# Inverting a running product from the product itself instead of scanning the inverses

## The chip, the cores and the metric

The kernel runs on one core of one Trainium2 chip. Its time is the device time of a run in microseconds; a profile of one execution tells where it goes. The engines are TensorE (PE, with its weight loads as PEld), VectorE (DVE), ScalarE (ACT), GpSimd (POOL) and SyncE (SP); transfers run on queues that SP, POOL and ACT issue to.

## The reference

A gated linear recurrence with complex gates feeds a feed-forward layer with a squared ReLU:

```
mag = sqrt(a_re^2 + a_im^2);  scale = min(mag, 0.999) / (mag + 1e-6)
a = (a_re + i a_im) * scale                       # per batch, head, step, channel
for t in range(S):
    S_t = a_t * S_(t-1) + k_t v_t^T               # S complex, 48 x 48 per head
    y_t = q_t . real(S_t)
x = y as (B*S, H*D)                               # 3072 x 384
out = relu(x @ w_in)^2 @ w_out                    # 384 -> 2048 -> 384
```

B = 4 batches, H = 8 heads, S = 768 steps, D = 48 channels, all in float32; the weights arrive as float64.

## The kernel before

**Algorithm.** With P_t the running product of the gates, the real part of q_t . S_t is a sum over s <= t of (q_t P_t)(k_s / P_s) v_s, so each unit becomes matrix products: q times P, k times 1/P, a masked score matrix, and a carried state. P starts from 2^59 in each sequence so that it stays in range over 768 steps. The kernel works in real numbers: 1/P is conj(P)/|P|^2, so what k needs beside the parts of P is 1/|P|^2.

**Units.** The 3072 steps are cut into `NU` = 6 units of 512 steps. A unit's operands lie as 128 partitions of four consecutive steps (`W` = 4), in two halves `z` of four heads. Units 0 and 1 are handled in groups of two heads (`apply(z, p, 1)`), later ones a half at a time (`apply(z, 0, 2)`).

**`chain(n)` of a unit.** `roots` and `normalise` compute 1/mag by Ln and Exp with a Newton step and scale the gates; `inner` multiplies the four steps of a partition into prefix products (VectorE). `totals` transposes each partition's last product on TensorE, `scan` multiplies over the partitions (VectorE), `back` transposes the result: `xn[:, 0]`, `xn[:, 1]` hold the product up to each partition. `inverse` computes 1/|prefix|^2 inside each partition (Square, Ln, Exp on ScalarE, a Newton step on VectorE); its last column goes through `factors`: a transposing matmul (line 1061), a scan of products along the partitions (`tensor_tensor_scan`, line 1082, with tests of growth and size at 1086 and 1090), a transposing matmul back (line 1104): `xn[:, 2]` is the running product of inverses. `twist` multiplies k by the inverse inside the partition (line 994). `apply` multiplies the prefixes by `xn` (1245, 1249), k by `xn[:, 2]` (1252), then forms the products for k and for q (1259). `gather` moves those for k by DMA (line 1299).

**`pairs(n)`.** For each pair of heads: transposes of q's and k's products (on TensorE through line 1358 in units 0 and 1, copied out by ScalarE at 1362; by VectorE and DMA later), scores (1376) with a mask (1379), state sums (1404, 1413, 1415), the mix with v (1428, 1432), its copy (1438) and DMA into `xT` (1446).

**`dense(n, grp)`.** First layer at line 1468, ReLU and square on ScalarE (1499, 1500), second layer at 1514 in unit 0; later units use line 1565 and combinations of `w2` blocks made once at 1555. The float64 weights are fetched in pieces and converted by ScalarE (795, 799) and VectorE (801, 805, 808) during unit 0.

**Order.** Each operation is recorded as a `step` with an engine, an assumed duration, reads, writes and a rank; `Plan.order` replays them greedily (an engine takes the ready step of lowest rank) and the program is emitted in that order. Each engine runs its own queue in order. Ranks: `DENSE` = 3, `CHAIN` = 2, `PAIR` = 1; a step of `ahead` comes just before the unit's other chain steps, `late` is the rank of the inverse and of `apply`. Accumulated sums (`sums`, `grow`, `total`) are tested in `verdict`; where a test fails, a general branch of the program computes everything anew.

Of the kernel before, what the change touches and what calls it, by code (L numbers as in the profile page):

```python
# [588 lines left out]
def fast_path(ctx, tc, q, k, v, a_re, a_im, moe_w_in, moe_w_out, out, flag):  # L589
# [6 lines left out]
    C = 128  # L596
# [13 lines left out]
    CUT = C // 2  # L610
# [32 lines left out]
    x = sb("x", NM * (C + 1)).rearrange("p (m c) -> p m c", m=NM)  # L643
    xe = sb("xe", NM)
    txs = [sb(f"tx{j}", 3 * 24).rearrange("p (r g) -> p r g", r=3) for j in range(2)]
    ce = sb("ce", 2 * NM).rearrange("p (r m) -> p r m", r=2)
    cx = sb("cx", NM)
    xn = sb("xn", 3 * DM).rearrange("p (r n) -> p r n", r=3)
# [15 lines left out]
    NS = 10  # L664
    sums = sb("sums", NU * NS).rearrange("p (n j) -> p n j", n=NU)
    grow = sb("grow", NU * 2 * NM).rearrange("p (n j m) -> p n j m", n=NU, j=2)
    total = sb("total", B * NM).rearrange("p (b m) -> p b m", b=B)
# [30 lines left out]
    pool.memset(col, 1.0)  # L698
    pool.memset(txs[0].rearrange("p r (m k) -> p r m k", k=8)[:, 0, :, 0], 1.0)
# [179 lines left out]
    def chain(n):  # L879
# [12 lines left out]
        def third(lo, hi):  # L892

            return [("xn", 2, i) for i in range(lo // 64, (hi + 63) // 64)]

        def roots(z):
# [11 lines left out]
            else:  # L908
# [6 lines left out]
                out=f0, in_=m2, func=AF.Ln), first)  # L915
# [10 lines left out]
        def normalise(z):  # L926
            f0, f1, _, t = col[z]
            step("ACT", ac(Y), key(z, 3), key(z, 0), lambda: act.activation(
                out=f0, in_=t, func=AF.Copy, scale=0.999), first)
            step("ACT", ac(Y), key(z, 3), key(z, 1), lambda: act.activation(  # L930
                out=f1, in_=t, func=AF.Copy, scale=-1e-6, bias=1.0), first)
            step("DVE", tt(Y), key(z, 0, 1), key(z, 0), lambda: dve.scalar_tensor_tensor(
                out=f0, in0=f0, scalar=1.0, in1=f1, op0=ALU.min, op1=ALU.mult), first)
            a2 = A[z].rearrange("p (r x) -> p r x", r=2)
            step("DVE", tt(Z), key(z, 0), [("a", z)], lambda: dve.tensor_tensor(  # L935
                out=a2, in0=a2, in1=f0.unsqueeze(1).to_broadcast([C, 2, Y]),
                op=ALU.mult), first)
            check("ACT", ac(Y), key(z, 3), [], lambda: act.activation(
                out=junk[:, 0:Y], in_=t, func=AF.Square, saturate=False,
                accum_out=sums[:, n, 2 + z:3 + z]), first)  # L940
            if n == 0:
                check("ACT", ac(Y), key(z, 2), [], lambda: act.activation(
                    out=junk[:, 0:Y], in_=col[z][2], func=AF.Copy, saturate=False,
                    accum_out=sums[:, n, z:z + 1]), first)
# [25 lines left out]

        def inverse(z):
            f0, f1, d, t = col[z]
            rk = late[z]
            step("ACT", ac(Z), [("a", z)], key(z, 0, 1), lambda: act.activation(
                out=ff[z][:, 0:Z], in_=A[z], func=AF.Square), rk)
            step("DVE", tt(Y), key(z, 0, 1), key(z, 2), lambda: dve.tensor_tensor(
                out=d, in0=f0, in1=f1, op=ALU.add), rk)
            step("ACT", ac(Y), key(z, 2), key(z, 0), lambda: act.activation(
                out=f0, in_=d, func=AF.Ln), rk)
            step("ACT", ac(Y), key(z, 0), key(z, 1), lambda: act.activation(  # L980
                out=f1, in_=f0, func=AF.Exp, scale=-1.0), rk)
            step("DVE", tt(Y), key(z, 1, 2), key(z, 3), lambda: dve.scalar_tensor_tensor(
                out=t, in0=d, scalar=-1.0, in1=f1, op0=ALU.mult, op1=ALU.mult), rk)
            step("DVE", tt(Y), key(z, 1, 3), key(z, 3), lambda: dve.scalar_tensor_tensor(
                out=t, in0=t, scalar=2.0, in1=f1, op0=ALU.add, op1=ALU.mult), rk)
            xh = xn.rearrange("p r (h d) -> p r h d", h=H)[:, :, ts(z, HH)]
            t4 = t.rearrange("p (h c d) -> p h c d", h=HH, c=W)
            step("ACT", ac(Y // W), key(z, 3), third(z * HH * D, (z + 1) * HH * D),
                 lambda: act.copy(out=xh[:, 2], in_=t4[:, :, W - 1]), rk)

        def twist(z):
            t = col[z][3]
            kk = QK[z][:, Y:2 * Y]
            step("DVE", tt(Y), key(z, 3) + [("qk", z)], [("k", z)], lambda: dve.tensor_tensor(
                out=kk, in0=kk, in1=t, op=ALU.mult), late[z])
# [54 lines left out]

        def factors(lo, hi, rk):

            rows = [(m, max(lo - C * m, 0), min(hi - C * m, C)) for m in range(lo // C, (hi - 1) // C + 1)]
            ks = third(lo, hi)
            b = trs[slot["tr"] % 2]
            ps = bank[b][:, 0:DM].rearrange("p (m t) -> p m t", m=NM)
            slot["tr"] += 2

            def go():
                for m, p0, p1 in rows:  # L1060
                    pe.matmul(ps[p0:p1, m], lhsT=xn[:, 2, C * m + p0:C * m + p1], rhs=ident,
                              start=True, stop=True)
            step("PE", 0.12 * len(rows), ks, [(b,)], go, rk)

            groups = [([m for m, p0, p1 in rows if (p0, p1) == (0, C)], 0, C)] + [
                ([m], p0, p1) for m, p0, p1 in rows if (p0, p1) != (0, C)]

            def scan_x():
                for ms, p0, p1 in groups:
                    if not ms:  # L1070
                        continue
                    sl = slice(ms[0], ms[-1] + 1)
                    if fresh:
                        dve.memset(x[p0:p1, sl, 0], SCALE ** -2)
                    else:
                        dve.tensor_copy(out=x[p0:p1, sl, 0], in_=cx[p0:p1, sl])
                    for hf in range(2):
                        t0, t1 = hf * CUT, (hf + 1) * CUT
                        if hf and cross:
                            dve.memset(x[p0:p1, sl, t0], SCALE ** -2)  # L1080
                        for m in ms:
                            dve.tensor_tensor_scan(
                                out=x[p0:p1, m, t0 + 1:t1 + 1], data0=ps[p0:p1, m, t0:t1],
                                data1=mask[p0:p1, 0:CUT], initial=x[p0:p1, m, t0:t0 + 1],
                                op0=ALU.mult, op1=ALU.bypass)
                        dve.scalar_tensor_tensor(
                            out=grow[p0:p1, n, hf, sl], in0=x[p0:p1, sl, t0], scalar=2.0 ** 124,
                            in1=x[p0:p1, sl, t1], op0=ALU.mult, op1=ALU.is_ge)
                        if (ends and hf) or (cross and not hf):
                            dve.tensor_scalar(  # L1090
                                out=total[p0:p1, ps_[0][2], sl], in0=x[p0:p1, sl, t1],
                                scalar1=2.0 ** 114, scalar2=None, op0=ALU.is_le)
                    if not ends:
                        dve.tensor_copy(out=cx[p0:p1, sl], in_=x[p0:p1, sl, C])
            kx = [("x", i) for _, _, i in ks]
            check("DVE", sum(0.5 + 0.6 * len(ms) for ms, _, _ in groups if ms), [(b,)] + kx, kx,
                  scan_x, rk)

            b2 = trs[(slot["tr"] + 1) % 2]
            ps2 = bank[b2][:, 0:DM]  # L1100

            def go2():
                for m, p0, p1 in rows:
                    pe.matmul(ps2[:, C * m + p0:C * m + p1], lhsT=x[p0:p1, m, 0:C],
                              rhs=ident[p0:p1, p0:p1], start=True, stop=True)
            step("PE", 0.12 * len(rows), kx, [(b2,)], go2, rk)
            step("ACT", ac(hi - lo), [(b2,)], ks, lambda: act.copy(
                out=xn[:, 2, lo:hi], in_=ps2[:, lo:hi]), rk)
# [106 lines left out]

        def squares(j):
            for r in range(2):
                check("ACT", ac(Y), [(("qk", "k")[r], j)], [], lambda r=r: act.activation(
# [7 lines left out]
        def apply(z, p, np):  # L1226
# [20 lines left out]
            for r, op in ((0, ALU.subtract), (1, ALU.add)):  # L1247
# [3 lines left out]
            lo = (z * HH + 2 * p) * D  # L1251
            step("DVE", tt(n1), third(lo, lo + nh * D), [("k", z)], lambda: dve.tensor_tensor(
                out=qk[:, 1], in0=qk[:, 1], in1=over(2), op=ALU.mult), late[z])
# [497 lines left out]
```

## Time and profile before

| | |
|---|---|
| median of 3 runs | 722.57 us (722.43 to 722.73) |
| span of the profiled execution | 722.6 us |
| PE busy | 647.1 us |
| weight loads busy | 579.3 us |
| DVE busy | 576.7 us |
| ACT busy | 359.1 us |
| POOL busy | 176.1 us |
| transfers | 79.53 MB, mean 110 GB/s |

The span runs from the first to the last instruction of one profiled execution; it is the only time that this execution has, and it equals the runs' median within 0.05 us. Busy times of PE come from pipelined records: a record's duration overlaps that of its neighbour, so the pace is read from starts or from the chain of waits. A float32 matmul appears as two records. Each engine runs its instructions in order, so an instruction that waits holds up all behind it.

### The profile page before, as it was taken

What the parts mean: (1) busy time and instruction counts of PE and PEld (TensorE: products, weight loads), DVE (VectorE), ACT (ScalarE), POOL (GpSimd) and SP (SyncE); (2) the same over time, 40 slices, a digit from 0 to 9 for tenths busy, and PEclk for the clock granted to TensorE, in tenths of its full rate; (3) what the DMA queues carried; (4) which work ended last, traced back from release to release, by engine and by line L of the source; (5) the groups of instructions that cost most, each with busy time, mean ns of one, the idle gap of its engine ahead of it and who ended that gap; (6) DMA issues with size and microseconds to landing.
All of it is one profiled execution on the core that took longest, in us unless ns stands there. A gap on an engine that the chain in (4) does not pass through costs nothing.

```text
span 722.6 us, 11635 instructions
## 1 busy us (share of the span) xinstructions
PE 647.1 (90%) x4118; PEld 579.3 (80%) x4118; DVE 576.7 (80%) x1188; ACT 359.1 (50%) x579; POOL 176.1 (24%) x333
## 2 busy tenths in 40 slices
PE   0017798999998999999999999999999999999996
PEld 0006687677777799999999899999998989999996
DVE  6998899799776589879799588999788997347621
ACT  6792557965366523347713559424569142122230
POOL 6504154051500003305006241024050033032100
PEclk9999899999998999999999999999999999999999
DMA  9732259220530002646006772017560045297400
GB/s 287 239 128 65 57 114 275 104 66 10 161 116 19 4 12 74 179 122 165 0 12 177 165 153 65 1 36 186 157 163 9 1 128 129 51 325 266 153 1 27
DMA packets 56356, 79.53 MB, mean 110 GB/s; under 512 B 10944, under 2 KB 38464, under 8 KB 56288
## 3 DMA queue, kind: packets, MB, share of 16 engines
q0 software_dynamic: 15232, 40.72, 18.7%
q1 hardware_dynamic: 36928, 32.98, 17.9%
q10 hardware_dynamic: 4128, 4.98, 2.6%
q8 instruction: 35, 0.57, 0.4%
q14 instruction: 33, 0.27, 0.1%
HBM read 48.76 MB, written 4.72 MB: 74 GB/s over the span
## 4 chain that ended last, share of the span: by engine, by line
PE 76%; DVE 14%; ACT 3%; DMA 2%; SPq 2%; issue 1%; POOL 0%; DVEq 0%
PE d L1468 29%; PE d L1565 26%; PE sc L1376 5%; PE d L1514 4%; PE tr L1404 3%; PE yp L1428 3%; DVE f L954 3%; PE yp L1432 2%; DVE aq L935 1%; PE tr L1013 1%; PE d L1358 1%; DMA KC<-f 1%; DVE f L1259 1%; DVE aq L960 1%; DVE f L1245 1%
## 5 line engine op out<-in xcount | busy, mean ns | idle before, releaser
L1468 PE MATMUL d<-xT,w 128*128 128x256 f32 x1056 | 236.9, 382 | 0.6 <-DMA xT<-yt 0.6
L1468 PEld LDWEIGHTS d<-xT,w 128*128 128x128 f32 x1056 | 199.3, 191 | 27.8 <-issue 1.1
L1565 PE MATMUL d<-w,g 128*128 128x192 f32 x768 | 132.2, 327 | 0.0
L1565 PEld LDWEIGHTS d<-w,g 128*128 128x128 f32 x768 | 124.9, 190 | 1.1 <-issue 0.7
L1499 ACT ACTIVATE g<-d 128x512 f32<-128x512 f32 x88 | 52.4, 595 | 127.0 <-PE d L1468 113.3
L1299 POOL DMA_DIRECT2D KC<-f x160 | 78.9, 501 | 121.7 <-DVE f L1259 55.9
L1580 DVE TENSOR_TENSOR g<-g 128x512 f32<-128x512 f32 x64 | 43.6, 688 | 35.4 <-ACT g L1500 20.3
L1565 PE MATMUL d<-T,g 128*128 128x192 f32 x384 | 66.8, 326 | 0.0
L875 POOL DMA_DIRECT2D v<-in_v_dram x80 | 46.5, 588 | 82.6 <-PE yp L1428 28.5
L1526 POOL DMA_DIRECT2D out_dram<-ot x22 | 12.4, 562 | 207.5 <-DVE ot L1589 136.0
L1565 PEld LDWEIGHTS d<-T,g 128*128 128x128 f32 x384 | 62.9, 190 | 0.0
L1500 ACT ACTIVATE g<-g 128x512 f32<-128x512 f32 x96 | 60.6, 631 | 3.1
L1376 PE MATMUL sc<-QT 96*128 96x128 f32 x368 | 49.9, 292 | 2.1 <-ACT QT L1362 2.1
L1376 PEld LDWEIGHTS sc<-QT 96*128 96x128 f32 x368 | 46.5, 204 | 4.9 <-ACT QT L1362 2.9
L1259 DVE TENSOR_TENSOR f<-aq 128x384 f32<-128x384 f32 (+1 forms) x64 | 45.1, 752 | 0.6
L1245 DVE TENSOR_TENSOR f<-aq,xn 128x384 f32<-128x384 f32 (+1 forms) x64 | 44.7, 748 | 0.0
L1514 PE MATMUL d<-w,g 128*128 128x384 f32 x128 | 43.3, 487 | 0.7 <-DVE w L808 0.7
L1438 ACT COPY yt<-yp 112x512 f32<-112x512 f32 x24 | 26.3, 1097 | 25.2 <-PE yp L1432 25.2
L1589 DVE TENSOR_TENSOR ot<-ot,d 128x192 f32<-128x192 f32 x64 | 21.7, 349 | 21.5 <-PE d L1565 21.1
L954 DVE TENSOR_TENSOR f<-aq 128x384 f32<-128x384 f32 x72 | 36.9, 553 | 0.9
L1514 PEld LDWEIGHTS d<-w,g 128*128 128x128 f32 x128 | 23.5, 190 | 15.2 <-DVE w L808 1.1
L1013 PE MATMUL tr<-perm,xn 128*128 128x128 f32 x36 | 6.1, 303 | 32.7 <-ACT xn L969 31.6
(194 smaller groups left out, 1019.5 us busy)
## 6 DMA issues: line engine op xcount, KB each, us to landing
QT<-aq SPq DMA_DIRECT2D x128, 64.0 KB, 2.1
f<-in_moe_w_in_dram POOLq DMA_DIRECT2D x8, 768.0 KB, 7.9
f<-in_moe_w_out_dram POOLq DMA_DIRECT2D x8, 768.0 KB, 6.4
KC<-f POOLq DMA_DIRECT2D x104, 48.0 KB, 2.2
out_dram<-ot POOLq DMA_DIRECT2D x22, 192.0 KB, 2.2
QT<-aq ACTq DMA_DIRECT2D x64, 64.0 KB, 2.3
v<-in_v_dram POOLq DMA_DIRECT2D x80, 48.0 KB, 2.7
xT<-yt SPq DMA_DIRECT2D x36, 96.0 KB, 2.4
```

Of the source, the lines that this page charges most:

```text
L875: lambda i=i, c=c, src=src: pool.dma_start(out=t[32 * c:32 * c + 32, i], in_=src[c]), vrank, 32 * 1536, 4.0,
L954: dve.tensor_tensor(out=f, in0=a[:, :, :, c - 1], in1=a[:, j, :, c].unsqueeze(1).to_broadcast([C, 2, HH, D]), op=ALU.mult)
L1245: lambda j=j, r=r: dve.tensor_tensor(out=f4[:, j, r], in0=a[:, r], in1=over(j), op=ALU.mult), late[z])
L1259: lambda j=j, r=r, o=o: dve.tensor_tensor(out=o[:, :, :, r * D:(r + 1) * D], in0=qk[:, j], in1=a[:, r], op=ALU.mult), late[z])
L1299: lambda i=i, c=c, queue=queue: queue.dma_start(out=kc[32 * c:32 * c + 32, i], in_=nat[32 * i:32 * i + 32, c]),
L1376: pe.matmul(sa[:, j], lhsT=T[:, j, 1, h], rhs=T[:, j, 0, h], start=True, stop=True)
L1468: pe.matmul(ps, lhsT=w1[:, f // FP, m, ts(f % FP, C)], rhs=xT[:, n % 2, m, ts(grp, G)], start=(m == 0), stop=(m == NM - 1))
L1499: act.activation(out=o, in_=ps, func=AF.Relu)
L1500: act.activation(out=o, in_=o, func=AF.Square)
L1514: pe.matmul(ps, lhsT=gt[:, f % 2, ts(i, C)], rhs=w2[:, f], start=(f == 0), stop=(f == NF - 1))
L1565: pe.matmul(bank[b][:, 0:DH], lhsT=g4[:, r, j], rhs=w(j), start=first and j == 0, stop=last and j == NT - 1)
L1580: step("DVE", tt(4 * C), gk(x0, h) + gk(x1, h), gk(o, h), lambda: dve.tensor_tensor(out=g4[:, o, sl], in0=g4[:, x0, sl], in1=g4[:, x1, sl] ...
```

## The change

The running product of inverses (`factors`, `inverse`, `twist`, the third row of `xn`) goes. Instead, `apply` inverts |P|^2 of the complete product, element by element, with its own Square, Ln, Exp and Newton step. To keep Ln and Exp in range, each partition has a level `lv`, one over the sum of the squares of its `xn` row, taken by a Square with accumulation and a reciprocal; Ln reads it as a scale, and the Newton step and the last multiplication of k carry it as well. In `roots` the factor 0.999 moves into Ln's scale, so that one of two Copies of `normalise` goes, and the other reads the Exp's result ahead of the Newton step. A check of unit 0 (the sum over `m2`) gets a later rank. The sums of squares of k are taken before k is scaled. The tests of `grow` and `total` are replaced by sums read out behind the new Exp.

```diff
         def roots(z):
...
             step("ACT", ac(Y), key(z, 2), key(z, 0), lambda: act.activation(
-                out=f0, in_=m2, func=AF.Ln), first)
+                out=f0, in_=m2, func=AF.Ln, scale=CLIP ** -2), first)
...
+            step("ACT", ac(Y), key(z, 1), key(z, 0), lambda: act.activation(
+                out=f0, in_=f1, func=AF.Copy, scale=-1e-6 / CLIP, bias=1.0), first)
             step("DVE", tt(Y), key(z, 2, 3), key(z, 3), lambda: dve.scalar_tensor_tensor(
-                out=t, in0=m2, scalar=-0.5, in1=t, op0=ALU.mult, op1=ALU.mult), first)
+                out=t, in0=m2, scalar=-0.5 * CLIP ** -2, in1=t, op0=ALU.mult, op1=ALU.mult), first)
...
         def normalise(z):
-            step("ACT", ac(Y), key(z, 3), key(z, 0), lambda: act.activation(
-                out=f0, in_=t, func=AF.Copy, scale=0.999), first)
-            step("ACT", ac(Y), key(z, 3), key(z, 1), lambda: act.activation(
-                out=f1, in_=t, func=AF.Copy, scale=-1e-6, bias=1.0), first)
-            step("DVE", tt(Y), key(z, 0, 1), key(z, 0), lambda: dve.scalar_tensor_tensor(
-                out=f0, in0=f0, scalar=1.0, in1=f1, op0=ALU.min, op1=ALU.mult), first)
+            step("DVE", tt(Y), key(z, 0, 3), key(z, 0), lambda: dve.scalar_tensor_tensor(
+                out=f0, in0=t, scalar=1.0, in1=f0, op0=ALU.min, op1=ALU.mult), first)
...
-        def inverse(z):
...
-        def twist(z):
...
-        def factors(lo, hi, rk):
...
+        step("ACT", ac(Y) + 0.2, [("xn", r, z) for r in range(2) for z in range(2)], [("tot",)],
+             lambda: act.activation(out=junk, in_=xn.rearrange("p r n -> p (r n)"),
+                                    func=AF.Square, scale=LOW, saturate=False,
+                                    accum_out=tot[:, n:n + 1]), ahead)
+
+        def level():
+            dve.reciprocal(out=lv[:, n, 0:1], in_=tot[:, n:n + 1])
+            dve.tensor_scalar(out=lv[:, n, 1:2], in0=lv[:, n, 0:1], scalar1=-UP * UP,
+                              scalar2=None, op0=ALU.mult)
+        check("DVE", 0.16, [("tot",)], [("lv", n)], level, ahead)
...
         def apply(z, p, np):
...
-            lo = (z * HH + 2 * p) * D
-            step("DVE", tt(n1), third(lo, lo + nh * D), [("k", z)], lambda: dve.tensor_tensor(
-                out=qk[:, 1], in0=qk[:, 1], in1=over(2), op=ALU.mult), late[z])
+            f0, f1, d, t = [own[:, i * n1:(i + 1) * n1] for i in range(4)]
+            pp = a.rearrange("p r h c d -> p r (h c d)")
+            step("ACT", ac(2 * n1), [("a", z)], kf[0], lambda: act.activation(
+                out=own[:, 0:2 * n1].rearrange("p (r x) -> p r x", r=2), in_=pp,
+                func=AF.Square, scale=UP), late[z])
+            step("DVE", tt(n1), kf[0], kf[1], lambda: dve.tensor_tensor(
+                out=d, in0=f0, in1=f1, op=ALU.add), late[z])
+            step("ACT", ac(n1), kf[1] + [("lv", n)], kf[0], lambda: act.activation(
+                out=f0, in_=d, func=AF.Ln, scale=lv[:, n, 0:1]), late[z])
+            check("ACT", ac(n1) + 0.1, kf[0], kf[0], lambda: act.activation(
+                out=f1, in_=f0, func=AF.Exp, scale=-1.0,
+                accum_out=sums[:, n, 10 + 2 * z + p:11 + 2 * z + p]), late[z])
+            step("DVE", tt(n1), kf[0] + kf[1], kf[1], lambda: dve.scalar_tensor_tensor(
+                out=t, in0=d, scalar=lv[:, n, 0:1], in1=f1, op0=ALU.mult, op1=ALU.mult), late[z])
+            step("DVE", tt(n1), kf[0] + kf[1], kf[1], lambda: dve.scalar_tensor_tensor(
+                out=t, in0=t, scalar=-2.0, in1=f1, op0=ALU.add, op1=ALU.mult), late[z])
+            step("DVE", tt(n1), kf[1] + [("qk", z)], [("k", z)],
+                 lambda: dve.scalar_tensor_tensor(
+                     out=qk[:, 1].rearrange("p h c d -> p (h c d)"), in0=t,
+                     scalar=lv[:, n, 1:2], in1=qk[:, 1].rearrange("p h c d -> p (h c d)"),
+                     op0=ALU.mult, op1=ALU.mult), late[z])
...
         def rest(*zs):
             for z in zs:
-                inverse(z)
-            factors(zs[0] * HH * D, (zs[-1] + 1) * HH * D, late[zs[0]])
-            for z in zs:
-                twist(z)
                 squares(z)
```

More of the change, by code (lines that the diff above doesn't have):

```diff
@@ L609, in fast_path @@
     G = L // 2
-    CUT = C // 2
+    UP = 2.0 ** 4
+    LOW = 2.0 ** -1
+    CLIP = 0.999
     Z = 2 * HH * W * D
@@ L663, in fast_path @@
     mask = sb("mask", C)
-    NS = 10
+    NS = 14
+    lv = sb("lv", NU * 2).rearrange("p (n j) -> p n j", n=NU)
+    tot = sb("tot", NU)
     sums = sb("sums", NU * NS).rearrange("p (n j) -> p n j", n=NU)
-    grow = sb("grow", NU * 2 * NM).rearrange("p (n j m) -> p n j m", n=NU, j=2)
-    total = sb("total", B * NM).rearrange("p (b m) -> p b m", b=B)
     odd = sb("odd", NF)
@@ L698, in fast_path @@
     pool.memset(col, 1.0)
+    pool.memset(sums, 0.0)
     pool.memset(txs[0].rearrange("p r (m k) -> p r m k", k=8)[:, 0, :, 0], 1.0)
@@ L943, in normalise @@
                     out=junk[:, 0:Y], in_=col[z][2], func=AF.Copy, saturate=False,
-                    accum_out=sums[:, n, z:z + 1]), first)
+                    accum_out=sums[:, n, z:z + 1]), (CHAIN, 0.2))
         def inner(z):
@@ L969, in inner @@
                  lambda: act.copy(out=xh[:, 0:2], in_=a[:, :, :, W - 1]), ahead)
-        def inverse(z):
[L972 to L989, printed above, removed]
-        def twist(z):
[L992 to L995, printed above, removed]
         for fn in (roots, normalise, inner):
@@ L1049, in totals @@
             step("DVE", 0.12, [("ce",)], [("e", j)], start, ahead)
-        def factors(lo, hi, rk):
[L1053 to L1108, printed above, removed]
@@ L1644, in collect @@
         def collect():
-            for lo, hi, top_ in ((0, 2, 60), (2, 4, 12), (4, NS, 20)):
+            for lo, hi, top_ in ((0, 2, 60), (2, 4, 12), (4, 8, 7), (8, 10, 20), (10, NS, 60)):
                 dve.tensor_scalar(out=ok[:, :, lo:hi], in0=sums[:, :, lo:hi],
                                   scalar1=2.0 ** top_, scalar2=None, op0=ALU.is_le)
+            wide = sums[:, :, 10:NS]
+            dve.tensor_tensor(out=wide, in0=wide, in1=lv[:, :, 1:2].to_broadcast([C, NU, NS - 10]),
+                              op=ALU.mult)
+            dve.tensor_scalar(out=wide, in0=wide, scalar1=-2.0 ** 118, scalar2=None,
+                              op0=ALU.is_ge)
+            dve.tensor_reduce(out=good[:, 1:2], in_=wide, axis=AXY, op=ALU.min)
             dve.tensor_reduce(out=good[:, 0:1], in_=ok, axis=AXY, op=ALU.min)
-            dve.tensor_reduce(out=good[:, 1:2], in_=grow, axis=AXYZ, op=ALU.min)
-            dve.tensor_reduce(out=good[:, 2:3], in_=total, axis=AXY, op=ALU.min)
             dve.tensor_reduce(out=most, in_=odd, axis=AX, op=ALU.max)
```

9 lines of the change are left out of this document (2 added, 7 removed).

## The prediction

> **What bounds the kernel now.** I read the page first: totals, the slices, the chain.
>
> ```profile
> span 722.6 us, 11635 instructions
> PE 647.1 (90%) x4118; PEld 579.3 (80%) x4118; DVE 576.7 (80%) x1188; ACT 359.1 (50%) x579; POOL 176.1 (24%) x333
> PE   0017798999998999999999999999999999999996
> DVE  6998899799776589879799588999788997347621
> PE 76%; DVE 14%; ACT 3%; DMA 2%; SPq 2%; issue 1%; POOL 0%; DVEq 0%
> ```
>
> The span, 722.6 us, stands at the median of the runs (722.57), so the sum is made against it. TensorE is idle for 75.5 us, nearly all of it early: in the first slices it does nothing while VectorE is full. The chain agrees: mostly PE, with a DVE part. Next the stages, as windows of PE alone (columns: stage, its length, PE busy with its records, granted clock, DMA share, GB/s).
>
> ```profile
> 0.00:103.70 103.70, 45.45 (x332) 0.97 0.51 150
> 103.70:135.00 31.30, 27.55 (x120) 1.00 0.76 208
> 135.00:213.00 78.00, 77.28 (x419) 1.00 0.34 92
> 213.00:222.00 9.00, 4.86 (x49) 0.99 0.09 23
> 222.00:232.00 10.00, 10.00 (x62) 0.67 0.01 2
> 232.00:253.00 21.00, 19.33 (x91) 1.00 0.04 9
> 253.00:715.60 462.60, 462.60 (x3053) 1.00 0.39 107
> ```
>
> So there are three regimes. Up to 103.7 us VectorE's unit 0 sets the pace. From 253 us PE never waits: there only PE's own work counts, and VectorE time saved is worth nothing. Between them lies one hole at 213 to 222 us.
>
> **PE's own work.** The change drops both transposing stages of the inverse's scan (`factors`, lines 1061 and 1104). How long they hold PE is read from the chain of waits (start, length), since a record's mean overlaps its neighbours.
>
> ```profile
> 168.24 0.67 PE tr L1061 x6
> 168.91 3.89 PE d L1468 x18
> 172.79 0.67 PE tr L1104 x6
> L1061 PE MATMUL tr<-ident,xn 128*128 128x128 f32 (+1 forms) x38 | 6.4, 300 | 1.5 <-ACT xn L989 1.5
> ```
>
> Six records each per unit (38 = 8 for unit 0 and 30 for five units), 0.67 + 0.67 us a unit. Units 1 to 5 run after 135 us, where PE is full: 5 x 1.34 = **6.7 us** come off the path. Nothing is added on PE. Unit 0's are in the part that VectorE bounds.
>
> **VectorE and ScalarE, whole kernel.** Groups of instructions (busy us, mean ns; then idle before):
>
> ```profile
> L994 DVE TENSOR_TENSOR aq<-aq,f 128x768 f32<-128x768 f32 x12 | 11.4, 954 | 0.2
> L982 DVE SCALAR_TENSOR_TENSOR f<-f 128x768 f32<-128x768 f32 x12 | 11.4, 952 | 5.3 <-ACT f L980 5.3
> L1252 DVE TENSOR_TENSOR aq<-aq,xn 128x384 f32<-128x384 f32 (+1 forms) x16 | 12.0, 751 | 0.0
> L1082 DVE TENSOR_TENSOR_SCAN x<-tr,x,mask 128x64 f32<-128x64 f32 (+1 forms) x38 | 11.1, 336 | 0.9
> L1259 DVE TENSOR_TENSOR f<-aq 128x384 f32<-128x384 f32 x32 | 16.0, 553 | 0.3
> L1086 DVE SCALAR_TENSOR_TENSOR grow<-x 128x3 f32<-128x3 f32 (+2 forms) x18 | 2.9, 161 | 0.6
> L930 ACT ACTIVATE f<-f 128x768 f32<-128x768 f32 x12 | 9.9, 828 | 0.0
> L989 ACT COPY xn<-f 128x192 f32<-128x192 f32 x12 | 4.2, 346 | 6.6 <-DVE f L984 6.4
> L1031 ACT ACTIVATE e<-tr 128x384 f32<-128x384 f32 x6 | 3.1, 511 | 0.0
> L1218 ACT ACTIVATION_READ_ACCUMULATOR junk<-aq 128x1 f32 x24 | 4.5, 187 | 0.0
> ```
>
> Gone from VectorE: the twist 11.4, the multiplication by the running inverse 12.0, scans 11.1 and their tests 2.9: 37.4 us. Added: one last scaled multiplication of k per group, as wide as L1252 (12.0), and twelve one-column operations (reciprocal, factor; nearest row 161 ns: 1.9). The three other operations of the inverse stay, but in units 0 and 1 cut in halves: 24 x 0.553 for 12 x 0.953, +1.8. Net -21.7 us. ScalarE: one Copy of two goes (9.9), L989 goes (4.2); the Square with a sum over xn comes (6 x (0.83 + 0.19) = 6.1) and 16 sums read out behind Exp (3.0): about -5 us. The reciprocal has no row; between 0.16 and 0.95 us each it moves unit 0 by under a microsecond, and I take 0.16. After 253 us all this is cover: PE has dense work queued.
>
> Ln now takes its scale from a tile, of which no row exists either. The Trainium skill ("ScalarE: Activation LUTs", What ACT_TABLE_LOAD costs) states some 93 ns more for such a pointer operand; by it unit 0's four Ln would end 0.4 us later in all, and no run here shows it.
>
> **Unit 0, where VectorE bounds.** Timeline rows of before (start, length, engine, line):
>
> ```profile
> 11.75 0.96 DVE L923 SCALAR_TENSOR_TENSOR f<-f 128x768 f32<-128x768 f32 x1
> 15.55 0.95 DVE L932 SCALAR_TENSOR_TENSOR f<-f 128x768 f32<-128x768 f32 x1
> 35.56 0.36 DVE L1122 TENSOR_TENSOR KC<-e 128x192 f32<-128x192 f32 x1
> 51.86 1.49 DVE L1245 TENSOR_TENSOR f<-aq,xn 128x384 f32<-128x384 f32 x3
> 57.63 1.96 DVE L1259 TENSOR_TENSOR f<-aq 128x384 f32<-128x384 f32 x4
> 59.65 3.65 PE L1358 MATMUL d<-ident,f 128*96 128x128 f32 x16 [3.55 <-DVE f L1259]
> 88.21 1.97 DVE L1259 TENSOR_TENSOR f<-aq 128x384 f32<-128x384 f32 x4
> 103.33 0.48 PE L1432 MATMUL yp<-QT,St 96*48 96x128 f32 x3
> 109.89 1.13 PE L1468 MATMUL sc<-xT,w 128*128 128x256 f32 x4 [2.27 <-DVE w L808]
> 118.30 1.13 PE L1468 MATMUL tr<-xT,w 128*128 128x256 f32 x4 [0.80 <-DVE w L808]
> ```
>
> *Normalisation.* The min (L932) waits until 15.55 for two Copies behind L923's end at 12.71; now its factor is ready before, so the half 0 gains 2.8 us. In the changed order half 1's two refining operations, which filled that hole, come later (2 x 0.95): half 1 gains 1.0. Ahead of the scan the order of VectorE then has parts of a second weight conversion (two operations of 0.9) where the two sums of squares stood: the scan starts at about 35.3 instead of 35.56. So no gain there yet, only weight work done earlier.
>
> *Apply.* The products with xn start at about 50.4 instead of 51.86 (L982, L984, L994 gone from before them, a conversion put there), and no inverse scan (4 x 0.336 + 4 x 0.161 = 2.0 us) interrupts them: the complete product is ready at about 53.8. Then the new serial part: Square 0.83, sum 0.55, Ln 0.51, Exp 0.51, read-out 0.19, three operations at 0.55 to 0.6: about 5 us with the handovers. Products of the other half-groups stand between, so VectorE does not idle, but the first gather can start only when k is scaled: the four L1259 begin at 59.7, 2.1 us later than 57.63, and PE's transposes at 61.7. VectorE's in-order queue then holds, behind each group's wait for Exp, the masks and state sums of the pair before, and PE waits for those; replayed group by group with these lengths, the last L1259 ends near 99.7 (before 90.18) and the last mix near 109.0 (before 103.8), **5.2 us later**.
>
> *What that delays.* PE's first dense layer. But VectorE has by then converted all of w1, since the changed order puts those conversions into the spaces: the waits of 2.27 and 0.80 us for conversions go. PE's changed order also has two matmuls of that layer ahead of the last mix (four records of 0.216 us, by L1468 x18: 0.86 us). 5.2 - 2.27 - 0.86 - 0.80 = 1.3; as w2's conversions come earlier too, I take another 0.8 off, an estimate by that last wait: **+0.5 us**. Ends: -3 (the trips to ScalarE hidden wholly) and +6 (the late start kept in full). SP's queue has transfers of xT of pair 1 inside half 1's gather; that is in the replay.
>
> *The rest.* The final check gets four short operations more and loses two; they and the one added clearing on GpSimd at the start stand where their engines idle (VectorE's slices are down to 2 and 1 tenths at the end), so nothing; uncovered, 4 x 0.16 us.
>
> **The hole at 213 us.** Rows of it, and one for comparison:
>
> ```profile
> 184.08 1.95 PE L1376 MATMUL sc<-QT 96*128 96x128 f32 x16
> 221.72 3.75 PE L1376 MATMUL sc<-QT 96*128 96x128 f32 x16 [1.44 <-ACT QT L1362]
> 225.82 4.20 PE L1468 MATMUL d<-xT,w 128*128 128x256 f32 x12
> ```
>
> PE idles 4.1 us of 9 while ScalarE has unit 2's work between the copies of unit 1's last pairs, and then runs at a granted 0.67: scores 3.75 instead of 1.95, dense 4.2 instead of 2.6 (12 x 0.216): 3.4 us more. Unit 1's chain now ends several us earlier on VectorE, so its pairs meet more dense work as cover; but ScalarE's order still has Squares and sums between the copies. I take half the idle, **-2.1 us**, and leave the slow part. The rows show the low clock right behind that idle, and whether half of it would still bring it on they cannot tell: that is a rival.
>
> **Sum.** 722.6 - 6.7 + 0.5 - 2.1 = 714.3, say **714 us**.
>
> **Rivals.** *The hole closes whole*: then 4.1 + 3.4 go, and the 1.7 us of idle at 232 to 253: 722.6 - 6.7 + 0.5 - 9.2 = 707. For it: less ScalarE and VectorE work ahead of it. Against: unit 2's Squares still stand between the copies. *Half the idle goes and the slow clock with it*: another 3.4 us off, 711. For it: in the windows the grant is low only behind that idle (0.67), and 1.00 before. Against: the granted clock fell after stalls of 1.5 us and less that stood close together, which may remain. The Trainium skill ("TensorE: Matmul & The Clock Gate", Part 1: The HAM clock gate) has the clock halve after about 3.4 us of idle, and by that rule this case would be the likely one. *Unit 0's trips to ScalarE become the bound*: each of the four half-groups stands on VectorE for Square, Ln, Exp and read-out (0.83 + 0.51 + 0.51 + 0.19 and handovers, about 2.5 us), 10 us in place of what I find hidden, a lag of some 12 us at the first dense layer: 722.6 - 6.7 + 12 = 728. It decides from a lag of 7 to 8 us on. For it: no spare VectorE work but conversions; against: the order puts other groups' products there. *PE only waits where it worked*: the transposes leave, but their place becomes a wait for the later gather or the return transposes: 722. Against: no PE wait at all after 253 us. That the final check sends the run into the general branch is under 1 in 100: the largest new sum for these inputs is near 2^115, its limit 2^118.
>
> **Numbers.** Forecast 0.48 (its own range 711 to 720: the front's two ends), slow clock gone as well 0.14, closed hole 0.13, ScalarE trips 0.16, waits for work 0.09. About 0.2% (1.4 us) is what a measurement tells from no change. Faster: 0.48 + 0.14 + 0.13 + 0.02 of the last = 0.77; same 0.05; slower 0.18. The range 707 to 723 leaves out the trips' case and the low part of the closed hole.
>
> **What would show it.** Right: no six-record groups of the inverse between dense matmuls; PE full from about 250 us to the end in some 455 us; first transposes of unit 0 near 62, last mix near 109, no wait for w1 conversions behind it. Wrong: last mix beyond 115 (trips), or PE waits on lines of the gather or the return transposes after 250 us.

## The result, and the profile after

The changed kernel takes **726.14 us** (725.83 to 726.46, 4 runs) beside 722.50 us (722.32 to 722.73) of the kernel before: a ratio of 1.005, 95% interval 1.0036 to 1.0064. It is slower by 3.6 us, where 8.6 us less had been forecast. The profiled execution has a span of 724.7 us. (A run's time lies about 1.75 us above its span, 726.46 for this one; so the 722.6 us of the span before belongs to a run of some 724, and spans are compared with spans below.)

The page, its totals and the slices of PE and VectorE:

```profile
span 724.7 us, 11426 instructions
PE 637.5 (88%) x4042; PEld 570.8 (79%) x4042; DVE 555.9 (77%) x1125; ACT 354.9 (49%) x588; POOL 176.2 (24%) x334
PE   0005779999999999986999999999999999999996
DVE  6999995798878597977796587897887979428721
PE 37%; DVE 1%; ACT 1%; DMA 0%; issue 0%; SPq 0%; DVEq 0%; ACTq 0%
```

The three busiest engines have less work: PE 9.6 us, VectorE 20.8, ScalarE 4.2. Yet the span is 2.1 us longer: PE's idle time rose from 75.5 to 87.2 us. (The chain is followed back over 40% of the span here and is nearly all PE there; it ends before it reaches what follows.) Where the idle time lies is seen in the same stages as before (stage, its length, PE busy, granted clock, DMA share, GB/s):

```profile
0.00:103.70 103.70, 35.86 (x259) 0.97 0.46 141
103.70:135.00 31.30, 29.89 (x163) 0.95 0.94 249
135.00:213.00 78.00, 76.74 (x416) 1.00 0.32 86
213.00:222.00 9.00, 8.96 (x79) 1.00 0.14 44
222.00:232.00 10.00, 10.00 (x67) 1.00 0.08 21
232.00:253.00 21.00, 21.00 (x114) 1.00 0.00 1
253.00:715.60 462.60, 452.71 (x2943) 0.99 0.39 107
```

Length less busy time, stage by stage against the rows before: up to 135 us +7.3; 135 to 213 us +0.5; 213 to 253 us -5.8, since the hole is gone and the slow clock behind it (0.67) with it; from 253 us on **+9.9**, where there had been none. PE's waits in that last stage (line, what it waited for: us, times, longest):

```profile
PE yp L1362 <- DVE A L1313: 3.6, 4, 1.1
PE d L1402 <- issue: 3.5, 1, 3.5
PE sc L1310 <- DVE A L1313: 1.3, 1, 1.3
PE d L1402 <- DVE ot L1523: 0.9, 1, 0.9
PE d L1402 <- DMA xT<-yt: 0.4, 1, 0.4
```

PE waits for the masks of scores (L1313) and for the first dense layer's input (L1402): it has pairs to do that are not ready, and no dense work left. For the wait of 3.5 us the profile names no releaser; the last pair's copy ends at 334.25 us, and its two transfers, issued at 334.3 and 334.8, take 2.4 to 3.2 us to land, so that they are its likely cause. In unit 2 that looks so (PE's timeline; start, length):

```profile
320.55 1.16 PE L1310 MATMUL sc<-QT 96*128 96x128 f32 x8 [1.34 <-DVE A L1313]
...
323.08 0.31 PE L1362 MATMUL yp<-A,v 128*48 128x128 f32 x1 [1.02 <-DVE A L1313]
...
327.09 0.39 PE L1362 MATMUL yp<-A,v 128*48 128x128 f32 x2 [0.96 <-DVE A L1313]
...
338.14 5.37 PE L1402 MATMUL d<-xT,w 128*128 128x256 f32 x16 [3.53 <-issue]
```

The pairs of unit 2 are late for the following reason. VectorE and ScalarE in its second half, first after, then before:

```profile
283.35 0.92 DVE L1169 TENSOR_TENSOR aq<-f 128x768 f32<-128x768 f32 x1
288.45 0.63 ACT L1434 ACTIVATE g<-g 128x512 f32<-128x512 f32 x1
288.66 1.29 DVE L1514 TENSOR_TENSOR g<-g 128x512 f32<-128x512 f32 x2 [4.40 <-PE d L1499]
...
289.01 1.48 ACT L1173 ACTIVATE f<-aq 128x1536 f32<-128x1536 f32 x1
291.40 0.94 DVE L1176 TENSOR_TENSOR f<-f 128x768 f32<-128x768 f32 x1
292.38 0.94 ACT L1178 ACTIVATE f<-f,lv 128x768 f32<-128x768 f32 x1 [1.89 <-DVE f L1176]
293.35 0.84 ACT L1180 ACTIVATE f<-f 128x768 f32<-128x768 f32 x1
294.42 1.01 DVE L1183 SCALAR_TENSOR_TENSOR f<-f,lv 128x768 f32<-128x768 f32 x1
295.95 0.95 DVE L1185 SCALAR_TENSOR_TENSOR f<-f 128x768 f32<-128x768 f32 x1
296.94 1.02 DVE L1188 SCALAR_TENSOR_TENSOR aq<-f,lv,aq 128x768 f32<-128x768 f32 x1
297.99 0.96 DVE L1197 TENSOR_TENSOR f<-aq 128x768 f32<-128x768 f32 x1
```

```profile
290.29 1.83 DVE L1249 TENSOR_TENSOR aq<-f 128x768 f32<-128x768 f32 x2
292.04 0.95 DVE L1252 TENSOR_TENSOR aq<-aq,xn 128x768 f32<-128x768 f32 x1
293.02 1.83 DVE L1259 TENSOR_TENSOR f<-aq 128x768 f32<-128x768 f32 x2
```

From the complete product (end at 284.27) to the first product of k (297.99) it takes 13.7 us, though the six operations of the inverse in it (Square, sum, Ln, Exp, two Newton operations) are 6.2 us by these rows: the Square (L1173) stands behind rectifiers (L1434) and starts 4.7 us late, the sum (L1176) stands behind state sums, and Ln, Exp and Newton follow in turn. VectorE is idle for 4.40 us of this, since the next instruction in its queue (L1514) waits for PE. Before, one multiplication stood there: 292.12 to 293.02, 0.9 us. The changed kernel reaches unit 2's totals 7.6 us earlier (250.61 to 243.02), but its pairs end 6.4 us later (325.40 to 331.82).

For all later units I take as one measure the **stretch** from the end of the return transposes on PE to the end of k's and q's last products on VectorE (timelines): before 28.4, 30.9, 34.1 and 31.1 us for units 2 to 5, mean 31.1; after 41.5, 40.4, 43.5 and 41.9, mean 41.8.

### The profile page after: what moved, and what is told of

Same layout as the page of the kernel before. It is cut to its first block, busy times and chain, and to the rows that moved or that the text cites. A ratio compares the mean times of both kernels' runs of the same rounds, so it can differ in the third digit from the quotient of the medians.

```text
span 724.7 us, 11426 instructions
## 1 busy us (share of the span) xinstructions
PE 637.5 (88%) x4042; PEld 570.8 (79%) x4042; DVE 555.9 (77%) x1125; ACT 354.9 (49%) x588; POOL 176.2 (24%) x334
## 5 line engine op out<-in xcount | busy, mean ns | idle before, releaser
L1402 PE MATMUL d<-xT,w 128*128 128x256 f32 x1056 | 238.4, 383 | 4.9 <-issue 3.5
L1402 PEld LDWEIGHTS d<-xT,w 128*128 128x128 f32 x1056 | 199.5, 191 | 33.7 <-issue 5.9
L1499 PEld LDWEIGHTS d<-w,g 128*128 128x128 f32 x768 | 125.2, 190 | 0.7 <-issue 0.4
L1434 ACT ACTIVATE g<-g 128x512 f32<-128x512 f32 x96 | 60.5, 631 | 3.0
L1514 DVE TENSOR_TENSOR g<-g 128x512 f32<-128x512 f32 x64 | 42.9, 683 | 24.0 <-ACT g L1434 14.0
L1310 PEld LDWEIGHTS sc<-QT 96*128 96x128 f32 x368 | 44.9, 198 | 6.8 <-ACT QT L1296 3.4
L1362 PE MATMUL yp<-A,v 128*48 128x128 f32 x320 | 36.1, 299 | 3.7 <-DVE A L1313 3.6
L1313 DVE TENSOR_TENSOR A<-sc,mask 128x512 f32<-128x512 f32 x45 | 30.0, 684 | 8.2 <-PE sc L1310 8.0
L1523 DVE TENSOR_TENSOR ot<-ot,d 128x192 f32<-128x192 f32 x64 | 21.7, 349 | 19.0 <-PE d L1499 18.6
```

The costliest lines, as they stand in the source:

```text
L1310: pe.matmul(sa[:, j], lhsT=T[:, j, 1, h], rhs=T[:, j, 0, h], start=True, stop=True)
L1362: pe.matmul(ypair[64 * h:64 * h + D, ts(j, C)], lhsT=v5[:, j, 2 * i + h], rhs=aa[h][:, j], start=True, stop=at[j] is None)
L1402: pe.matmul(ps, lhsT=w1[:, f // FP, m, ts(f % FP, C)], rhs=xT[:, n % 2, m, ts(grp, G)], start=(m == 0), stop=(m == NM - 1))
L1434: act.activation(out=o, in_=o, func=AF.Square)
L1499: pe.matmul(bank[b][:, 0:DH], lhsT=g4[:, r, j], rhs=w(j), start=first and j == 0, stop=last and j == NT - 1)
L1514: step("DVE", tt(4 * C), gk(x0, h) + gk(x1, h), gk(o, h), lambda: dve.tensor_tensor(out=g4[:, o, sl], in0=g4[:, x0, sl], in1=g4[:, x1, sl] ...
```

## The experiments

"Trip" below means the inverse's steps behind the complete product: Square, sum, Ln, Exp, two Newton operations. On the chips of these runs the kernel before scattered more (719.7 to 726.1 us) than in the first comparison. Each ratio is to runs of the kernel before that were taken beside the experiment's.

**1. The change in two parts.** In the first, `roots` and `normalise` of the changed kernel in the kernel before; in the second, those of before in the changed kernel.

> The kernel before with only the edit of the normalisation (0.999 in Ln's scale, one Copy fewer). Theory T (the loss comes from the inverse's trip to ScalarE, which now stands between the complete product and the products for k, in units 2 and on): 721 to 723 us, since unit 0's scan starts no earlier. Rival R (the changed normalisation reorders ScalarE and loses): 724 to 727 us.

722.52 us, ratio 1.0002 (0.9982 to 1.0022): the normalisation alone does nothing, and R's 724 us are not reached.

> The changed kernel with the normalisation of before. Theory T: 725 to 728 us, all of the loss stays. Rival R: 720 to 723 us.

730.12 us, ratio 1.0104 (1.0061 to 1.0147), 2 us above T's range. The loss belongs to the inverse, and R is out. The normalisation, worth nothing alone, seems to give some 4 us back beside it; the intervals of the two ratios (1.0061 to 1.0147, and 1.0036 to 1.0064 with it) just touch.

**2. Without the scan, without the trip.**

```diff
 # the first, on the kernel before
-            factors(zs[0] * HH * D, (zs[-1] + 1) * HH * D, late[zs[0]])
-                 lambda: act.copy(out=xh[:, 2], in_=t4[:, :, W - 1]), rk)
+                 lambda: act.mul(out=xh[:, 2], in_=t4[:, :, W - 1], mul=SCALE ** -2), rk)
 # the second, on the changed kernel: Square to the scaling of k go
+            step("DVE", tt(n1), [("a", z), ("qk", z)], [("k", z)], lambda: dve.scalar_tensor_tensor(
+                out=qk[:, 1], in0=qk[:, 1], scalar=SCALE ** -2, in1=qk[:, 0], op0=ALU.mult, op1=ALU.mult), late[z])
```

> The kernel before without the running product of inverses: both transposing matmuls, the scans and their tests are left out (k gets the last column of the inverse inside the partition, times 2^-118). The rest of the inverse stays where it was, beside the scan of P. Theory T: PE's 6.7 us come off and more, 712 to 716 us, PE full after 250 us. Rival W (PE waits in the place of the work that is taken out): 720 to 723 us.

> The changed kernel without the inverse of the complete product: Square, sum, Ln, Exp and the two Newton operations are left out, k is multiplied by a constant and by q in one operation. The level (tot, lv) stays. Theory T: 708 to 714 us, no PE wait in 300 to 340 us. Rival L (the loss is a bad order, whatever the chain's length): 720 us or more, waits elsewhere.

706.85 us, ratio 0.978 (0.9737 to 0.9823), and 697.41 us, ratio 0.9663 (0.9618 to 0.9709): both gain more than T said, and W and L are out. The first keeps an inverse with the same Square, Ln, Exp and Newton step, but takes it early, beside the running product: it is 19 us faster than the changed kernel with 3.4 us more of VectorE work (559.3 against 555.9 us) and the same number of PE's records (4042), and PE does not wait after 253 us. So it is not the amount of the trip's work that costs, but where it stands.

**3. Where.** The trip left out in units 2 to 5 alone (`if n < 2:` around it, a multiplication of k by a constant and q in its place), then in units 0 and 1 alone.

> The changed kernel with the trip of the inverse (Square, sum, Ln, Exp, Newton step) left out in units 2 to 5 alone, where k is multiplied by a constant and by q in one instruction in its place; units 0 and 1 keep it, so the values of units 2 to 5 are not the reference's. Theory T (what the changed kernel loses, it loses in the later units, where the trip stands between the complete product and k's products and PE runs out of dense work): PE's 9.9 us of idle after 253 us go, and 708 to 716 us are left. Rival F (the loss is in the front, where unit 0 now makes PE wait 12.5 us for k's first products): 718 to 726 us, with the idle after 253 us changed by less than 3 us.

> The changed kernel with the trip left out in units 0 and 1 alone, and kept in units 2 to 5; the values of units 0 and 1 are not the reference's. T: the front gives back up to 9 us of unit 0's wait, but the later units still wait, and as the front runs ahead they run out of dense work the sooner: 714 to 722 us, 8 us or more of idle after 253 us. F: 700 to 712 us.

710.05 us, ratio 0.9827 (0.9781 to 0.9872), and 708.64 us, ratio 0.9811 (0.9766 to 0.9856). PE from 253 us on, in the first and in the second:

```profile
253.00:700.00 447.00, 446.81 (x2939) 1.00 0.40 110
```

```profile
253.00:700.00 447.00, 438.60 (x2856) 0.99 0.40 110
```

The idle time goes with the late units' trip (0.2 us) and stays with it (8.4), as T has it. Of the 15.2 us between the spans of the changed kernel and the first (724.7 and 709.5), 9.7 are PE's idle time after 253 us, 1.8 its idle time before, and 3.7 its busy time. But T had given the second kernel 714 us or more: units 0 and 1 pay as much for the trip as the later ones, and F was right on that time. The trip thus costs in two places, about 16 us in the late units and 17 in the first two, and what the change saves elsewhere hides most of it.

**4. The order.** Ranks alone are changed. First, every step from the complete product to k's scaling goes ahead of all else in units 1 to 5:

```diff
-                         in0=f4[:, 0, r], in1=f4[:, 1, 1 - r], op=op), late[z])
+                         in0=f4[:, 0, r], in1=f4[:, 1, 1 - r], op=op), (late[z] if n == 0 else (-1, n)))
 # the same for the products with xn and for the trip
```

> The changed kernel with every step from the complete product to k's scaling put ahead of all other work of its engines in units 1 to 5 (both halves' products and trips before the first half's products of k, and ahead of the rectifiers on ScalarE); nothing is left out. T with an order that can mend it (the trip is late because half 1's product and its Square stand behind half 0's work and behind rectifiers): 712 to 720 us, and half 1's trip in unit 2 takes under 9 us where it took 13.7. Rival (the trip is too long whatever its rank, or what is put behind it is missed elsewhere): 723 to 732 us.

746.93 us, ratio 1.0329 (1.0261 to 1.0398), the worst of all and above even the rival's range, though the stretch falls to a mean of 33.3 us and the waits for masks from 4.9 us to 0.3. PE's longest waits after 253 us:

```profile
PE d L1499 <- DVE ot L1523: 9.0, 3, 7.4
PE d L1499 <- DVE g L1514: 8.3, 2, 7.6
```

What was put behind the trip, the combinations of the second dense layer's operands and its sums (1514, 1523), is what PE needs at once. Then the trip's steps alone, on ScalarE (`late[z]` to `(-1, n)` at 1173, 1178, 1180), and on both engines:

> The changed kernel with only ScalarE's four steps of the trip (Square, Ln, Exp, in all units) ahead of the rectifiers and copies that stood before them in ScalarE's order; VectorE's steps keep their rank. Nothing is left out. Theory Q (the trip is long because its ScalarE steps queue behind rectifiers and copies): 716 to 722 us. Rival P (what is put behind them is missed by PE's dense work at once, as when the product and the whole trip went first): 726 us or more.

> As the kernel with ScalarE's steps first, with VectorE's four steps of the trip first too, while the complex products keep their rank; in unit 0, where the second quarter's trip was broken up by other work (its last step ended 12 us after its product), it now runs through. Nothing is left out. Q: 714 to 722 us. P: 726 us or more.

727.18 us, ratio 1.0059 (1.0037 to 1.0082), and 721.24 us, ratio 0.998 (0.9962 to 0.9998). ScalarE's steps alone do nothing, as P has it. With VectorE's steps too, 5 us come back, within Q's range, and the kernel is level with the one before. They come back in the front: unit 0's last products end at 89.3 us instead of 98.9, and PE idles 65.7 us up to 253 us instead of 70.5, but still 9.4 us behind it. None of the three orders takes the late idle time away: it is 20.2 us in the first, 9.9 and 9.4 in the others.

**5. What in the late trip.** Two copies more, ScalarE's steps out, the Newton operations out, each in units 2 to 5 alone:

```diff
 # the first
+            for _ in range(2 if n >= 2 else 0):
+                step("ACT", ac(n1), kf[0], kf[0], lambda: act.activation(out=f1, in_=f1, func=AF.Copy), late[z])
 # the second: Square, Ln and Exp only `if n < 2`, k scaled by a constant and q behind the rest
 # the third: both Newton operations only `if n < 2`, k scaled by Exp's result
```

> The changed kernel with two more ScalarE copies in place (about 0.84 us each) between the Exp and the Newton step in each half of units 2 to 5: the trip becomes some 1.7 us longer at each of eight places, 13 us of ScalarE work in all, on an engine that is busy 49% of the span. Nothing is left out. T (the length of the trip in the later units is paid by PE): 4 to 13 us above the changed kernel, so 730 to 739 us. Rival C (after 253 us the trip is covered by PE's dense work, as the prediction had it, and the 4 us come from elsewhere): within 2 us of 726.1.

> The changed kernel with ScalarE's three steps of the trip (Square, Ln, Exp) left out in units 2 to 5; VectorE's three operations (sum, two of the Newton step) still run there in the same place, on what lies in the buffers, and k is then multiplied by a constant and q, behind them. The values of units 2 to 5 are not the reference's. Theory X (the handovers to ScalarE and back hold the late units up): 709 to 714 us, and under 3 us of idle after 253 us, as without the trip there (710.05). Rival D (VectorE's added operations between the complete product and k's scaling hold them up): 718 to 726 us.

> The changed kernel without the two VectorE operations of the Newton step in units 2 to 5: k is scaled by Exp's result itself (there with the opposite sign and the accuracy of Ln and Exp); ScalarE's steps and the sum stay. X: 721 to 726 us, with 6 us or more of idle after 253 us. D: 711 to 718 us.

726.89 us, ratio 1.0073 (1.0049 to 1.0096); 715.40 us, ratio 0.9887 (0.9851 to 0.9924); 716.58 us, ratio 0.9925 (0.9893 to 0.9957). Against T, longer costs next to nothing (C's number); shorter by either part gains about 10 us. The kernel without ScalarE's steps lies 1.4 us above X's range, the one without Newton's in D's, so neither X nor D alone holds. What goes with the idle time of these kernels is how long the whole way is, not what stands on it. Mean stretch, PE's idle time from 253 us to its last matmul, and time, for kernels that have the same steps in units 0 and 1:

| kernel | stretch | idle | time |
|---|---|---|---|
| trip in units 0 and 1 only | 27.7 us | 0.2 us | 710.05 us |
| no ScalarE steps late | 34.4 | 1.2 | 715.40 |
| no Newton operations late | 36.1 | 5.7 | 716.58 |
| changed kernel | 41.8 | 9.9 | 726.14 |
| two copies more | 44.4 | 12.4 | 726.89 |

Some 34 us are nearly free here; beyond, PE runs out of dense work. The curve is uneven (9.6 us of time from 36.1 to 41.8, and 0.8 to 44.4), and I have no account of that: each kernel has an order of its own. The stretch is no measure where the order itself starves PE: with products and trip first, 33.3 us go with 20.2 us of idle time.

**6. What an order's accidents are worth.** One number of the greedy order, the margin on PE's waits, from 0.6 to 0.9 us, in both kernels:

```diff
-    MARGIN = 0.6
+    MARGIN = 0.9
```

> The changed kernel, nothing left out, with one number of the greedy order changed: the margin that it adds to PE's waits, 0.9 instead of 0.6 us. It tells what the order's accidents are worth. Theory T (the trip holds the late units up in any order of this kind): 722 to 731 us, and the distance to the kernel before with the same margin stays positive. Rival O (0.5% is the luck of one order): the two kernels change places, or the distance moves by more than 5 us.

> The kernel before, nothing left out, with the same margin of 0.9 us. T: 718 to 727 us, below the changed kernel with that margin. O: above it, or the distance moves by more than 5 us.

728.12 us, ratio 1.0083 (1.0056 to 1.0109), and 726.54 us, ratio 1.0053 (1.003 to 1.0076). Each moves by 2 to 4 us, as much as the change's whole effect; the order between the two stays, but these intervals overlap. The mechanism does not move: stretches of 41.8 and 30.6 us, and 9.4 and 2.6 us of idle time behind 253 us. O, which needed a change of places or 5 us, is out. So the late wait is the change's; that the balance comes out at +0.5% and not at zero is partly this one order.

**7. A version that beats both.** The inverse of the running product is taken from the product itself, but of the 384 values per partition that `xn` has, not of the complete product's 768 in each half; the inverse inside a partition stays early, as before. The scan and its transposes go, and the normalisation is the changed kernel's. The lines below are the calls alone, without the steps that record them.

```diff
-            factors(zs[0] * HH * D, (zs[-1] + 1) * HH * D, late[zs[0]])
 # behind `back`, all with rank `ahead`; s0, s1, d are parts of KC[0]
+        act.activation(out=KC[0][:, 0:2 * DM], in_=xn[:, 0:2], func=AF.Square, scale=LOW, accum_out=tot[:, n:n + 1])
+        # lv = 1 / tot, and -LOW^2 / tot; d = s0 + s1
+        act.activation(out=s0, in_=d, func=AF.Ln, scale=lv[:, n, 0:1])
+        act.activation(out=s1, in_=s0, func=AF.Exp, scale=-1.0, accum_out=sums[:, n, 10:11])
+        # d = (d * lv * s1 - 2) * s1;  xn[:, 2] = d * (-LOW^2 * lv)
```

> The kernel before with its scan of inverses and the two transposing stages replaced by an inverse of the running product itself: its 384 squared magnitudes through a tile-scaled Ln, Exp and one Newton step beside the complex products, while the inverse of the product within a partition is taken early as before; the normalisation is the changed kernel's. Nothing is left out. T (the position of the trip decides, not the scan and not the trip's work): the trip runs beside work that waits for something else, and the time is 706 to 712 us, near the 706.9 us of the kernel without any factors. Rival W (a Ln, an Exp and a Newton step cost their own time wherever they stand): 718 us or more.

**714.34 us** (712.08 to 714.60), ratio 0.9878 (0.9831 to 0.9926): faster than both kernels, above T's range and below W's. It does not wait late, although VectorE has 17.7 us more to do than in the changed kernel (573.6 against 555.9 us). PE from 253 us on, and VectorE and ScalarE in unit 2's first half:

```profile
253.00:700.00 447.00, 446.67 (x2936) 1.00 0.40 110
```

```profile
266.98 0.55 DVE L1162 TENSOR_TENSOR KC<-KC 128x384 f32<-128x384 f32 x1
267.45 0.95 DVE L1204 TENSOR_TENSOR f<-aq,xn 128x768 f32<-128x768 f32 x1
267.62 0.61 ACT L1164 ACTIVATE KC<-KC,lv 128x384 f32<-128x384 f32 x1 [0.95 <-DVE KC L1162]
268.27 0.52 ACT L1166 ACTIVATE KC<-KC 128x384 f32<-128x384 f32 x1
268.43 0.96 DVE L1208 TENSOR_TENSOR aq<-f 128x768 f32<-128x768 f32 x1
269.31 0.61 DVE L1168 SCALAR_TENSOR_TENSOR KC<-KC,lv 128x384 f32<-128x384 f32 x1
...
271.96 0.95 DVE L1211 TENSOR_TENSOR aq<-aq,xn 128x768 f32<-128x768 f32 x1
```

Ln and Exp run on ScalarE from 267.62 to 268.79 us, while VectorE makes the complex products (1204, 1208) that k needs anyway; nothing waits for them. The stretch is 33.7 us, PE's work 636.5 us, and its idle time 76.3 us, about that of before (75.5): the 9.8 us between the two spans are PE's busy time.

## Why the prediction was wrong, point by point

**PE's own work: right.** 76 records went; PE's busy time fell by 9.6 us. The 6.7 us of the units 1 to 5 and the 3.4 us that the slow clock had added at 222 us make 10.1; the new slow places (last section) take a part back. Busy time is not set by the records alone: kernels with the same 4042 records are busy for 625.0 us (no trip, mean granted clock 0.996) to 646.3 us (products and trip first, 0.967). The version of experiment 7 has the gain beside an idle time like that of before: 6.9 us between the medians (721.27 and 714.34).

**VectorE and ScalarE, whole kernel: sizes right, conclusion wrong, and this is the step that failed.** -21.7 was -20.8 us and -5 was -4.2. But "After 253 us all this is cover" priced the trip by its work. The edit takes work away and makes the way from the running product to k's products longer, by 10.7 us on average in units 2 to 5; PE was full there only as long as pairs came before the dense work was used up. The term was put at nothing and came out at 9.9 us of idle time. That PE never waits after 253 us was read as a property of the stage; it was a reserve of unknown size. The trace of before had the number that should have warned: 0.9 us between complete product and k's products, where six dependent operations more were to be put. The rival "PE only waits where it worked", at 722 us and 0.09, is the nearest to what happened, with the wrong lines: the masks and the dense input wait, not the gather or the return transposes.

**Ln with a scale from a tile.** Now there is a row. ScalarE's groups after, by form (busy, mean ns, then idle before):

```profile
L1178 ACT ACTIVATE f<-f,lv 128x768 f32<-128x768 f32 x8 | 7.4, 930 | 8.3 <-DVE f L1176 8.3
L1180 ACT ACTIVATE f<-f 128x768 f32<-128x768 f32 x8 | 6.7, 843 | 0.3
```

Ln with the tile's scale takes 87 ns more than the Exp behind it on the same shape; the Trainium skill's 93 ns ("ScalarE: Activation LUTs", What ACT_TABLE_LOAD costs) agrees, and unit 0's four Ln, of half this width, came to some 0.35 us more (611 against 524 ns each). The reciprocal took 0.16 us, as assumed.

**Unit 0: the lateness was mis-sized.** The first four products of k began at 61.11 us (59.7 predicted, 57.63 before), the last group's ended at 98.85 (99.7): the replay was right. The unit's last mix ended at 112.5 us, not 109.0, since I let it follow 9.3 us behind the last products, where both kernels need 13.6 (before: 90.18 to 103.8). That is +8.7 us instead of +5.2. The two waits for w1's conversions did go. Against the +0.5 us that the forecast had for all of this, PE's idle time up to 213 us grew by 7.8. Where the time went is seen in the second group: complete product ready at 64.95 us, k's products from 73.68 on, with conversions, state sums and masks between the trip's steps.

```profile
62.99 1.96 DVE L1169 TENSOR_TENSOR aq<-f 128x384 f32<-128x384 f32 x4
...
65.33 0.55 DVE L1176 TENSOR_TENSOR f<-f 128x384 f32<-128x384 f32 x1
...
68.54 0.61 DVE L1183 SCALAR_TENSOR_TENSOR f<-f,lv 128x384 f32<-128x384 f32 x1
...
69.82 0.55 DVE L1185 SCALAR_TENSOR_TENSOR f<-f 128x384 f32<-128x384 f32 x1
...
73.04 0.60 DVE L1188 SCALAR_TENSOR_TENSOR aq<-f,lv,aq 128x384 f32<-128x384 f32 x1
73.68 1.96 DVE L1197 TENSOR_TENSOR f<-aq 128x384 f32<-128x384 f32 x4
```

"ScalarE trips" as a rival was thus half right, and its 728 us are the nearest to the time: they cost there, and the second kernel of experiment 3 shows how much (some 17 us less than the changed kernel without the trip in units 0 and 1). But they do not decide alone, and that 728 came so close is in part luck, since it holds neither the late wait nor the closed hole.

**The hole at 213 us: the closed hole, a rival with 0.13, was right.** 5.8 us of idle time and the slow clock went, where 2.1 had been taken. Whether the lead that this gave PE brought it to the end of its dense work sooner, and so added to the late waits, no run shows.

**The sum.** 722.6 - 9.6 (work) + 7.3 + 0.5 (front) - 5.8 (hole) + 9.9 (late units) - 0.2 (the end without PE) = 724.7. The forecast lacked the last 9.9 and had too little in the front; its two errors in the good direction, the hole and the work, were smaller. (Both are spans; as the time of a run, the forecast's 714 would stand for some 716.)

## What to carry to other kernels

Price an edit on a chain by the latency between its two ends as well as by the engines' work: a dependent trip to another engine that looks small (six operations, 6.2 us) was most of 13.7 us in queues shared with other work. An engine that never waits has a reserve, and the profile here did not show how large it was; versions with the chain cut by one part and another did. If an inverse or another slow function is needed, take it of the smallest operand and as early as its input exists, beside work that is needed anyway: that kept PE's gain here. Another order is no sure cure: the trip alone put ahead by rank made up for the loss in unit 0, and the products put ahead with it lost 3%.

## What the runs showed of the hardware

The granted clock fell here after short stalls that stood close together as well as after a longer one (windows of PE, columns as before). After the four waits of 1.34, 1.02, 0.96 and 1.05 us between 319 and 329 us, PE ran at 0.62 for three microseconds, and after the single one of 3.53 us at 0.68 for about five:

```profile
329.00:332.00 3.00, 3.00 (x29) 0.62 0.22 37
332.00:334.60 2.60, 2.60 (x12) 1.00 0.52 94
338.10:343.40 5.30, 5.26 (x17) 0.68 1.09 281
343.40:350.00 6.60, 6.60 (x35) 1.00 0.13 26
```

The Trainium skill ("TensorE: Matmul & The Clock Gate", A second HAM failure mode: psum-queue depth-cycling) tells of a kernel in which frequent short idles between groups of matmuls made the clock fall and rise again; the rows agree, and give a case of four stalls of about 1 us within 9 us. A scalar_tensor_tensor on VectorE with a scale from a tile took 1,016 ns on 128x768 (line 1183, group) where one with a constant took 955 (line 921): 61 ns more.
